# Token and channel mixer on one core: normalisation in the transposed layout, and a token product in 14 matmuls instead of 15

## Chip, cores and metric

The kernel runs on one core of one Trainium2 chip. The metric is device microseconds (us) of one execution, as the median of several runs; lower is better. The engines are named as the profile names them: PE (TensorE matmuls), PEld (TensorE weight loads), DVE (VectorE), ACT (ScalarE), POOL (GpSimd) and SP (SyncE, which here only issues DMAs).

## What is computed

Inputs are `q, k, v` of shape (8, 8, 576, 64): batch, heads, tokens, head size. The model width is 8 x 64 = 512.

```python
q_s = softmax over the head size of q;  k_s = softmax over the tokens of k
kv  = einsum('bhsd,bhse->bhde', k_s, v)
x   = einsum('bhsd,bhde->bhse', q_s, kv), heads side by side   # (8, 576, 512)
h   = max(x^T @ w_tok1, 0) @ w_tok2;   u = x + h^T              # over the tokens
y   = u + max(u @ w_ch1, 0) @ w_ch2                             # first channel layer, 512 -> 1536 -> 512
mu, var = mean and variance of y over the 512 channels
xn  = (y - mu) / sqrt(var + 1e-6) * g_ln
out = y + max(xn @ w2_ch1, 0) @ w2_ch2                          # second channel layer, 512 -> 2048 -> 512
```

The weight matrices come as 64-bit floats; the kernel turns them into 32-bit ones on the chip ("decode").

## The kernel before, in words

**Precision.** Every large product is made in three passes: an operand is split into a rounded part (hi) and the rest (lo), and hi·hi, hi·lo and lo·hi are summed (`PASSES`, L18). `split` (L136) makes the two parts: ACT copies to the rounded type, and DVE or POOL subtracts.

**Units.** A unit is one batch with two heads; there are 32. The 576 tokens of a unit lie as 4 chunks of 128 rows and a tail of 64 rows. `Unit.start` (L409) gives each step a tick. `q_split` (L507) makes hi and lo of the normalised q: one ACT copy and one POOL subtraction over 128 x 640. `tok1` (L533) is the token product of q with `w_tok1`: 3 passes x 5 chunks = 15 matmuls (L538), where the fifth chunk is the tail with 64 empty rows. `q_T` (L545) transposes q; for the 8 early units it transposes the hi and lo parts, and the tail takes two transposes (L570).

**Blocks.** The 4608 tokens are worked in 9 blocks of 512. Blocks 0 to 7 of the first channel layer (`Phase1`) are the first 512 tokens of a batch; block 8 is made of the eight 64-token tails. A block runs over 12 slices of the hidden width; each is 12 matmuls into a PSUM tile (`L1`, L684), a ReLU with split (ACT L141, DVE L142) and 12 matmuls into four accumulators (`L2`, L701), two slices later. The second channel layer (`Phase2`) does the same with 16 slices (L829 and L844). `finish` (L708) adds the residual into `yT`, which has channels on the partitions and tokens along the row: 4 DVE additions (L722), 4 POOL additions (L725). `y_store` (L628) turns `yT` chunk by chunk with 4 transposes on PE (L631), copies on ACT (L641), and writes to the DRAM tensor `y_dram`, which is in the order of the tokens.

**Norm.** For block j of the second layer `Norm` (L743) loads 512 consecutive tokens of `y_dram` with tokens on the partitions (L740), takes mean and variance with `bn_stats` and `bn_aggr` on DVE (L768, L770), the reciprocal root with a few small operations (L775 to L789), normalises on DVE (L793, four tensor_scalar), and then makes four turns: each turn is 4 transposes on PE (L804) into a PSUM tile, from which ACT (L809) writes the hi part and DVE (L810) the lo part, both scaled with g_ln. So there are 9 x 4 = 36 turns.

```python
later(at, self.load)
for i in range(CT // 2):
    later(at + 4 + i, call(self.stats, i))
    later(at + 9 + i, call(self.hat, i))
...
for kk in range(KD):
    later(at + turns + kk + kk // 2, call(self.turn, kk))
```

**Order of the work.** The order on each queue is written out by hand. `tick()` advances a counter, and `later(n, fn)` puts a step n ticks ahead. In the first layer a slice has four ticks, in the second two (after L1 and after L2), so a block of the second layer has about 32 ticks. The Norm of block 0 is started in the last block of the first layer, that of block j + 1 in block j. The weights of the second layer are decoded in 32 chunks (`Loads`, L259), 8 in the block before the last one of the first layer, the others up to the end of block 0 of the second layer: per chunk one SP load, four DVE operations (L100, L108, L115, L121), one on ACT (L129) and one on POOL (L130). The blocks of the second layer run 0 to 8. At their end `finish` (L851) adds the residual and POOL issues the output's DMA (SP for the last block).

Of the kernel before, what the change touches and what calls it, by code (L numbers as in the profile page):

```python
# [24 lines left out]
def kernel(  # L25
# [44 lines left out]
    CT = BLK // P  # L70
    LAG = 2
# [9 lines left out]
    y_dram = dram.tile([NT, DM], F32, name="y_dram")  # L81
# [54 lines left out]
    def split(x, hi, lo, engine):  # L136
        nc.scalar.activation(out=hi, in_=x, func=AF.Copy)  # L137
        engine.tensor_tensor(out=lo, in0=x, in1=hi.bitcast(F32), op=ALU.subtract)  # L138
# [71 lines left out]
    def tok1_chunk(c0, n, rows):  # L210
        def load():
            st = stage(n * T)[:rows]
            if c0 < NC:
                src = w_tok1[0:S0].rearrange("(p c) t -> p c t", c=NC)[:, c0:c0 + n]
            else:
                src = w_tok1[S0:S].rearrange("(p c) t -> p c t", c=1)
            nc.sync.dma_start(out=st.rearrange("p (c t) w -> p c (t w)", c=n), in_=src)
            return st

        def use(st):  # L220
            return decode(
                st, lambda x: x.rearrange("p (c t) -> p c t", c=n),
                w1[:rows, 0, c0:c0 + n], w1[:rows, 1, c0:c0 + n],
            )
# [176 lines left out]
    class Unit:  # L401
# [143 lines left out]
        def q_T(self, i):  # L545
# [18 lines left out]
            w = (c1 - c0) * P  # L564
            for xs in ((0, 1),) if 2 * w <= 512 else ((0,), (1,)):
                pq = psum("pq", True)
                for x in xs:
                    for c in range(c0, c1):
                        m = (x - xs[0]) * w + (c - c0) * P
                        nc.tensor.transpose(  # L570
                            out=pq[:, m:m + P].bitcast(F32R), in_=self.qn[:, x, c],
                            identity=spare[3][:, IDR:IDR + P],
                        )
                nc.scalar.activation(
                    out=self.qT[:, xs[0]:xs[-1] + 1, sl],
                    in_=pq[:, 0:len(xs) * w].rearrange("p (x s) -> p x s", x=len(xs))[:, :, 0:n],
                    func=AF.Copy,
                )
# [49 lines left out]
    def y_store(j, c):  # L628
# [13 lines left out]
        if j < B:  # L642
            dst = y_dram[j * S:j * S + S0, :].rearrange("(p c) d -> c p d", c=NC)[c]
            nc.scalar.dma_start(out=dst, in_=yn)
            return
        for i in range(P // R):
            b = c * (P // R) + i
            nc.scalar.dma_start(out=y_dram[b * S + S0:(b + 1) * S, :], in_=yn[i * R:(i + 1) * R])
# [7 lines left out]
    class Phase1:  # L656
# [51 lines left out]
        def finish(self):  # L708
# [19 lines left out]

            for c in range(CT):
# [7 lines left out]
    def load_y(j, pool):  # L737
        y = pool.tile([P, CT, DM], F32, tag="y", name="y")
        src = y_dram[j * BLK:(j + 1) * BLK, :]
        nc.sync.dma_start(out=y, in_=src.rearrange("(p c) d -> p c d", c=CT))  # L740
        return y

    class Norm:  # L743
        def __init__(self, j):
            self.j = j

        def start(self, at, turns=12):
# [4 lines left out]
            for i in range(CT // 2):  # L752
                later(at + 4 + i, call(self.stats, i))
                later(at + 9 + i, call(self.hat, i))
            later(at + 6, self.root)
            later(at + 8, self.rstd)
# [3 lines left out]
        def load(self):  # L760
            self.y = load_y(self.j, w2p[0])

        def stats(self, i):
            if i == 0:
                self.st = main.tile([P, CT, 6], F32, tag="st6", name="st6")
                self.mv = main.tile([P, CT, 2], F32, tag="mv", name="mv")
            for c in range(2 * i, 2 * i + 2):
                nc.vector.bn_stats(out=self.st[:, c], in_=self.y[:, c])  # L768
            for c in range(2 * i, 2 * i + 2):
                nc.vector.bn_aggr(out=self.mv[:, c], in_=self.st[:, c])  # L770

        def root(self):
            self.ve = main.tile([P, CT], F32, tag="ve", name="ve")
            self.r = main.tile([P, CT], F32, tag="r0", name="r0")
            nc.vector.tensor_scalar(  # L775
                out=self.ve, in0=self.mv[:, :, 1], scalar1=1e-6, scalar2=None, op0=ALU.add
            )
            later(1, lambda: nc.scalar.activation(out=self.r, in_=self.ve, func=AF.Sqrt))

        def rstd(self):  # L780
            ve, r0 = self.ve, self.r
            r1 = main.tile([P, CT], F32, tag="r1", name="r1")
            nc.vector.reciprocal(out=r0, in_=r0)
            nc.vector.tensor_tensor(out=r1, in0=r0, in1=r0, op=ALU.mult)
            nc.vector.tensor_tensor(out=r1, in0=r1, in1=ve, op=ALU.mult)
            nc.vector.tensor_scalar(
                out=r1, in0=r1, scalar1=-0.5, scalar2=1.5, op0=ALU.mult, op1=ALU.add
            )
            nc.vector.tensor_tensor(out=r0, in0=r0, in1=r1, op=ALU.mult)  # L789
# [243 lines left out]
```

## Time and profile before

| | us |
|---|---|
| median of 3 runs | 1674.12 (1673.66 to 1674.39) |
| the profiled execution | 1673.57 |
| span of its profile, first to last instruction | 1671.8 |
| PE busy in the span | 1642.0 (98%) |
| DVE, ACT, POOL busy | 644.3, 410.1, 318.5 |

The first 94 us are the early units; the first channel layer follows, with the other units between its matmuls, until about 855 us, and then the second layer. "Busy" counts the time in which an engine has at least one instruction at work. The chain of work that ended last is followed back from the last instruction of the kernel, at each step to what released it.

### The profile page before, as it was taken

The page shows a single profiled execution, that of the slowest core. Times are in us where ns is not written, and L with a number is a line of the kernel's source. Part 1 is how long each engine was busy: PE and PEld are TensorE (multiplying, and loading weights), DVE is VectorE, ACT ScalarE, POOL GpSimd, SP SyncE. Part 2 cuts the span into 40 slices and gives each one's busy share as a digit, 9 for nine tenths or more (in the row PEclk, how much of TensorE's full clock was granted, in tenths as well). Part 3 has the DMA queues.
Part 4 walks back from the last instruction along what each step waited for, and adds up shares of the span by engine and source line. Part 5 has one row for each costly group of instructions (what it writes and reads, how often), then busy time and mean ns, then how long its engine had stood idle before and what let it go on. Part 6 is the DMA issues. An engine that isn't in the chain of part 4 may idle for free.

```text
span 1671.8 us, 20195 instructions
## 1 busy us (share of the span) xinstructions
PE 1642.0 (98%) x8136; PEld 1380.9 (83%) x8136; DVE 644.3 (39%) x1290; ACT 410.1 (25%) x824; POOL 318.5 (19%) x244
## 2 busy tenths in 40 slices
PE   5999999999999999999999999999999999999998
PEld 4888888888888888888888888888888888888887
DVE  6875434344333434353557621222223131222211
ACT  4663333323232323321222211111111111111110
POOL 5743522232232313221223200000000000000000
PEclk9999999999999999999999999999999999999999
DMA  8552312121121212133225210101010101010010
GB/s 230 126 159 75 87 49 69 49 53 51 42 68 28 76 36 69 28 107 114 88 86 173 76 44 25 51 25 51 25 51 25 51 17 60 0 69 8 5 46 26
DMA packets 122062, 105.39 MB, mean 63 GB/s; under 512 B 92976, under 2 KB 101424, under 8 KB 118512
## 3 DMA queue, kind: packets, MB, share of 16 engines
q1 hardware_dynamic: 115568, 86.27, 17.9%
q10 hardware_dynamic: 5248, 9.44, 1.6%
q0 software_dynamic: 1152, 8.39, 1.2%
q8 instruction: 64, 1.05, 0.3%
q14 instruction: 30, 0.25, 0.0%
HBM read 82.05 MB, written 22.02 MB: 62 GB/s over the span
## 4 chain that ended last, share of the span: by engine, by line
PE 94%; DVE 2%; POOL 1%; issue 1%; ACT 1%; DMA 1%; SPq 0%; POOLq 0%; DVEq 0%; ACTq 0%
PE ph L829 24%; PE acc L844 24%; PE ph L684 17%; PE acc L701 17%; PE pu L601 4%; PE pg L538 3%; PE pk L514 2%; PE py L631 1%; PE px L804 1%; PE pq L559 1%; PE pq L586 1%; DMA rawq<-in_q 0%; DVE spare L138 0%; DVE dt L108 0%; POOL yT L725 0%
## 5 line engine op out<-in xcount | busy, mean ns | idle before, releaser
L142 DVE SCALAR_TENSOR_TENSOR h<-ph,h 128x512 fp32r<-128x512 f32 x252 | 174.0, 691 | 708.8 <-ACT h L141 708.7
L829 PE MATMUL ph<-xT,w 128*128 128x512 f32 x1728 | 420.2, 392 | 0.0
L844 PE MATMUL acc<-w,h 128*128 128x512 f32 x1728 | 420.0, 392 | 0.0
L829 PEld LDWEIGHTS ph<-xT,w 128*128 128x128 f32 x1728 | 323.0, 188 | 70.5 <-POOL w L130 0.2
L844 PEld LDWEIGHTS acc<-w,h 128*128 128x128 f32 x1728 | 322.9, 188 | 68.9
L141 ACT ACTIVATE h<-ph 128x512 fp32r<-128x512 f32 x252 | 150.5, 597 | 770.7 <-PE ph L829 587.0
L684 PE MATMUL ph<-u,w 128*128 128x512 f32 x1296 | 324.7, 395 | 0.0
L701 PE MATMUL acc<-h,w 128*128 128x512 f32 x1296 | 323.7, 394 | 0.0
L701 PEld LDWEIGHTS acc<-h,w 128*128 128x128 f32 x1296 | 237.1, 188 | 46.7
L684 PEld LDWEIGHTS ph<-u,w 128*128 128x128 f32 x1296 | 236.8, 188 | 46.7 <-DVE u L621 0.4
L859 POOL DMA_DIRECT2D out<-y x8 | 4.4, 556 | 635.8 <-DVE y L855 635.8
L467 POOL TENSOR_TENSOR qt<-rawq,qm 128x640 f32<-128x640 f32 x24 | 30.3, 1261 | 241.0 <-PE pt L461 95.5
L130 POOL TENSOR_TENSOR w<-t,w 128x512 fp32r<-128x512 f32 x32 | 41.9, 1310 | 152.8 <-ACT w L129 152.8
L538 PE MATMUL pg<-w,qn 128*128 128x256 f32 x480 | 63.8, 285 | 3.4 <-ACT w L137 3.4
L538 PEld LDWEIGHTS pg<-w,qn 128*128 128x128 f32 x480 | 62.0, 193 | 6.0 <-ACT w L137 3.7
L601 PE MATMUL pu<-w,hs 128*128 128x288 f32 x384 | 61.4, 295 | 0.0
L601 PEld LDWEIGHTS pu<-w,hs 128*128 128x128 f32 x384 | 54.4, 188 | 0.3 <-ACT hs L141 0.2
L138 DVE TENSOR_TENSOR qT<-pq,qT 128x512 fp32r<-128x512 f32 (+1 forms) x48 | 22.0, 458 | 76.1 <-ACT qT L137 76.1
L725 POOL TENSOR_TENSOR yT<-yT,u 128x512 f32<-128x512 f32 x32 | 43.0, 1359 | 37.9 <-DVE yT L722 37.9
L482 POOL TENSOR_TENSOR kt<-rawk,kb 128x640 f32<-128x640 f32 x24 | 38.1, 1587 | 40.8 <-ACT kb L478 40.8
L138 POOL TENSOR_TENSOR qn<-qt,qn 128x640 fp32r<-128x640 f32 x24 | 38.0, 1582 | 32.7 <-ACT qn L137 30.9
L129 ACT ACTIVATE w<-t 128x512 fp32r<-128x512 f32 x32 | 20.3, 633 | 97.0 <-DVE t L121 94.6
(140 smaller groups left out, 1243.3 us busy)
## 6 DMA issues: line engine op xcount, KB each, us to landing
y<-y_dram SPq DMA_DIRECT2D x18, 1024.0 KB, 4.8
st<-in_moe_w_ch SPq DMA_DIRECT2D x31, 512.0 KB, 3.8
vt<-in_v SPq DMA_DIRECT2D x64, 128.0 KB, 2.9
y_dram<-yn ACTq DMA_DIRECT2D x32, 256.0 KB, 2.4
out<-y POOLq DMA_DIRECT2D x8, 1024.0 KB, 4.1
rawk<-in_k SPq DMA_DIRECT2D x54, 128.0 KB, 2.8
rawq<-in_q SPq DMA_DIRECT2D x27, 256.0 KB, 3.1
stage<-in_moe_w_ch SPq DMA_DIRECT2D x10, 512.0 KB, 3.8
```

The source lines that it names most:

```text
L130: nc.gpsimd.tensor_tensor(out=lo, in0=x, in1=hi.bitcast(F32), op=ALU.subtract)
L138: engine.tensor_tensor(out=lo, in0=x, in1=hi.bitcast(F32), op=ALU.subtract)
L141: nc.scalar.activation(out=hi, in_=x, func=AF.Relu)
L142: nc.vector.scalar_tensor_tensor(out=lo, in0=x, scalar=0.0, in1=hi.bitcast(F32), op0=ALU.max, op1=ALU.subtract)
L482: nc.gpsimd.tensor_tensor(out=self.kt, in0=self.kr, in1=kb.to_broadcast([P, NC + 1, 2, D]), op=ALU.subtract,)
L538: nc.tensor.matmul(out=pg[:, 0:T], lhsT=self.qn[:, x, c], rhs=w1[:, y, c, :], start=(n == 0), stop=(n == len(terms) - 1),)
L601: nc.tensor.matmul(out=pu[:, 0:HN], lhsT=l, rhs=r, start=(n == 0), stop=(n == len(terms) - 1))
L684: nc.tensor.matmul(out=ps, lhsT=w[:, x, kk, fo:fo + P], rhs=u[:, y, kk], start=(n == 0), stop=(n == 3 * KD - 1),)
L701: nc.tensor.matmul(out=self.acc[dd], lhsT=w[:, x, f % 2, dd * P:(dd + 1) * P], rhs=h[:, y], start=(f == self.f0 and n == 0), stop=(f == se ...
L725: nc.gpsimd.tensor_tensor(out=yT[:, :, x], in0=yT[:, :, x], in1=u[:, 1, :, x].bitcast(F32), op=ALU.add)
L829: nc.tensor.matmul(out=ps, lhsT=w[:, x, kk, fo:fo + P], rhs=xT[:, y, kk], start=(n == 0), stop=(n == 3 * KD - 1),)
L844: nc.tensor.matmul(out=self.acc[c], lhsT=h[:, x, c * P:(c + 1) * P], rhs=w[:, y, f % 2], start=(f == 0 and n == 0), stop=(f == self.f1 - 1 ...
```

## The change

`tok1` and its tail. The 64 rows of the tail chunk that were empty now take the lo part of the tail: rows 0 to 63 hold hi, rows 64 to 127 hold lo, and the hi part of the tail of `w_tok1` is loaded a second time into rows 64 to 127. One matmul gives hi·hi + lo·hi of the tail, a second gives hi·lo, so a unit has 3 x 4 + 2 = 14. `q_split` is one ACT copy, a POOL subtraction over 128 x 512 and one over 64 x 128. An early `q_T` transposes the tail once.

Norm. `y_store` takes mean and variance from each stored chunk (`bn_stats`, `bn_aggr` on DVE, in the blocks of the first layer) into a tile `mr` that holds them for all 9 blocks. `yT` itself is stored to a DRAM tensor `yT_dram` (1 MB per block, an SP DMA 8 ticks after `finish`). A new class `Root` makes the reciprocal roots for several blocks at once (blocks 0 to 6 in block 7 of the first layer, blocks 7 and 8 in block 0 of the second), turns `mr` with one PE transpose, and stores it as rows to `mr_dram`. `Norm` loads `yT` and, in two halves of 256 tokens, mean and reciprocal root as rows sent to all 128 partitions; per half, DVE subtracts (128 x 1024) and POOL multiplies (128 x 1024). A turn is then only the ACT copy and the DVE operation, from SBUF. The second layer keeps the first layer's blocks, in the order 0 to 6, 8, 7; `y_dram` is laid out by block, and block 8 is written to the output by two DMAs of 64 partitions.

```diff
+    y_dram = dram.tile([NB, P, CT, DM], F32, name="y_dram")
+    yT_dram = dram.tile([NB, P, KD, BLK], F32, name="yT_dram")
+    mr_dram = dram.tile([NB, 2 * BLK], F32, name="mr_dram")
+    mr = main.tile([P, NB, 2, CT], F32, name="mr")
...
+            for r in (slice(0, R), slice(R, P)):
+                nc.sync.dma_start(
+                    out=st[r].rearrange("p t w -> p (t w)"), in_=w_tok1[S0:S]
+                )
...
-            split(self.qt, self.qn[:, 0], self.qn[:, 1], nc.gpsimd)
+            split(self.qt, self.qn[:, 0], self.qn[:, 1, 0:NC], nc.gpsimd)
+            nc.gpsimd.tensor_tensor(
+                out=self.qn[R:, 0, NC], in0=self.qt[:R, NC],
+                in1=self.qn[:R, 0, NC].bitcast(F32), op=ALU.subtract,
+            )
...
-            terms = [(x, y, c) for x, y in PASSES[0:2] for c in range(NC + 1)]
-            terms += [(1, 0, c) for c in range(NC + 1)]
+            terms = [(x, y, c) for x, y in PASSES for c in range(NC)] + [(0, 0, NC), (0, 1, NC)]
...
+        nc.scalar.dma_start(out=y_dram[j, :, c], in_=yn)
+        st = main.tile([P, 6], F32, tag="st6", bufs=2, name="st6")
+        nc.vector.bn_stats(out=st, in_=yn)
+        nc.vector.bn_aggr(out=mr[:, j, :, c], in_=st)
...
+            later(8, lambda: nc.sync.dma_start(out=yT_dram[self.j], in_=yT))
...
+    class Root:
+        def start(self, at):
+            for n, fn in zip((0, 1, 2, 3), (self.root, self.rstd, self.turn, self.store)):
+                later(at + 2 * n, fn)
...
+        def turn(self):
+            n = (self.j1 - self.j0) * 2 * CT
+            pm = psum("pm")
+            nc.tensor.transpose(
+                out=pm[:n, 0:P],
+                in_=mr[:, self.j0:self.j1].rearrange("p j x c -> p (j x c)"), identity=ident,
+            )
+            self.rows = main.tile([P, P], F32, tag="mrr", name="mrr")[:n]
+            nc.scalar.activation(out=self.rows, in_=pm[:n, 0:P], func=AF.Copy)
...
     class Norm:
...
             later(at, self.load)
+            for i in range(2):
+                later(at + 4 * i, call(self.load_b, i))
+                later(at + 4 * i + 4, call(self.hat, i))
             for kk in range(KD):
                 later(at + turns + kk + kk // 2, call(self.turn, kk))
...
+        def load_b(self, i):
+            self.b = w2p[0].tile([P, 2, HB], F32, tag="mrb", name="mrb")
+            src = mr_dram[self.j].rearrange("(x n) -> x n", x=2)[:, i * HB:(i + 1) * HB]
+            nc.sync.dma_start(out=self.b, in_=src.partition_broadcast(P))
+
         def hat(self, i):
-            for c in range(2 * i, 2 * i + 2):
-                nc.vector.tensor_scalar(
-                    out=self.y[:, c], in0=self.y[:, c], scalar1=self.mv[:, c, 0:1],
-                    scalar2=self.r[:, c:c + 1], op0=ALU.subtract, op1=ALU.mult,
-                )
+            y = self.y[:, :, i * HB:(i + 1) * HB]
+            mu, r = (self.b[:, x:x + 1].to_broadcast([P, KD, HB]) for x in range(2))
+            nc.vector.tensor_tensor(out=y, in0=y, in1=mu, op=ALU.subtract)
+            nc.gpsimd.tensor_tensor(out=y, in0=y, in1=r, op=ALU.mult)
...
         def turn(self, kk):
...
-            pt = psum("px")
-            for c in range(CT):
-                nc.tensor.transpose(
-                    out=pt[:, c * P:(c + 1) * P],
-                    in_=self.y[:, c, kk * P:(kk + 1) * P], identity=ident,
-                )
-            g = gT[:, kk:kk + 1]
-            nc.scalar.activation(out=self.xT[:, 0, kk], in_=pt, func=AF.Copy, scale=g)
+            g, y = gT[:, kk:kk + 1], self.y[:, kk]
+            nc.scalar.activation(out=self.xT[:, 0, kk], in_=y, func=AF.Copy, scale=g)
             nc.vector.scalar_tensor_tensor(
-                out=self.xT[:, 1, kk], in0=pt, scalar=g, in1=self.xT[:, 0, kk].bitcast(F32),
+                out=self.xT[:, 1, kk], in0=y, scalar=g, in1=self.xT[:, 0, kk].bitcast(F32),
                 op0=ALU.mult, op1=ALU.subtract,
             )
...
-        for j in range(NB):
+        ORDER = [*range(B - 1), B, B - 1]
+        for j in ORDER:
...
+                        Root(0, B - 1).start(30)
...
-                    later(16, o.load)
-                    if o.j + 1 < NB:
-                        Norm(o.j + 1).start(14 if o.j == 0 else 8)
+                    later(18, o.load)
+                    if o.j == 0:
+                        Root(B - 1, NB).start(26)
+                    if o.j != ORDER[-1]:
+                        Norm(ORDER[ORDER.index(o.j) + 1]).start(15 if o.j == 0 else 8)
```

## Rows read from the trace of the kernel before

**Rows 1.** The page: busy time of each engine, and the granted TensorE clock in 40 slices.

```profile
PE 1642.0 (98%) x8136; PEld 1380.9 (83%) x8136; DVE 644.3 (39%) x1290; ACT 410.1 (25%) x824; POOL 318.5 (19%) x244
...
PEclk9999999999999999999999999999999999999999
```

**Rows 2.** The page: the chain that ended last, its shares by line.

```profile
PE ph L829 24%; PE acc L844 24%; PE ph L684 17%; PE acc L701 17%; PE pu L601 4%; PE pg L538 3%; PE pk L514 2%; PE py L631 1%; PE px L804 1%; PE pq L559 1%; PE pq L586 1%; DMA rawq<-in_q 0%; DVE spare L138 0%; DVE dt L108 0%; POOL yT L725 0%
```

**Rows 3.** Busy time by stretch: us, then PE, PEld, DVE, ACT, POOL (instructions), clock, DMA share, GB/s.

```profile
20.00:40.00 20.00, 14.71 (x88) 13.54 (x88) 15.67 (x38) 12.42 (x29) 16.52 (x14) 1.00 0.91 264
60.00:80.00 20.00, 17.56 (x150) 17.07 (x149) 17.12 (x42) 13.19 (x34) 14.96 (x11) 1.00 0.57 147
438.00:532.00 94.00, 94.00 (x521) 81.06 (x520) 37.48 (x85) 28.77 (x64) 27.82 (x20) 1.00 0.21 53
853.00:943.00 90.00, 90.00 (x411) 73.88 (x410) 67.14 (x110) 23.48 (x42) 28.09 (x21) 1.00 0.43 135
1391.00:1481.00 90.00, 90.00 (x404) 73.93 (x403) 21.81 (x42) 12.32 (x21) 0.53 (x1) 1.00 0.10 36
```

**Rows 4.** The chain in a late block: start, us, what; first and last of the turns.

```profile
1539.83 2.72 PE ph L829 x12
1542.55 0.44 PE px L804 x4
...
1558.02 2.04 PE ph L829 x9
```

**Rows 5.** Groups of instructions on PE: busy us, mean ns, idle before.

```profile
L538 PE MATMUL pg<-w,qn 128*128 128x256 f32 x480 | 63.8, 285 | 3.4 <-ACT w L137 3.4
...
L804 PE MATMUL px<-ident,y 128*128 128x128 f32 x144 | 21.6, 272 | 0.0
```

**Rows 6.** The chain in the first layer: a unit's token product, and one single transpose.

```profile
194.89 1.77 PE pg L538 x15
...
200.85 0.11 PE pt L461
```

**Rows 7.** The chain at the early units' end: token product, tail transposes, first layer.

```profile
87.47 1.73 PE pg L538 x15
...
91.54 0.12 PE pq L570 x2
...
94.32 0.69 PE ph L684 x3
```

**Rows 8.** Groups on POOL: busy us, mean ns, idle before and its releaser.

```profile
L130 POOL TENSOR_TENSOR w<-t,w 128x512 fp32r<-128x512 f32 x32 | 41.9, 1310 | 152.8 <-ACT w L129 152.8
...
L138 POOL TENSOR_TENSOR qn<-qt,qn 128x640 fp32r<-128x640 f32 x24 | 38.0, 1582 | 32.7 <-ACT qn L137 30.9 <-DMA rawq<-in_q 1.8
...
L138 POOL TENSOR_TENSOR w<-more,w 128x128 fp32r<-128x128 f32 x1 | 0.5, 467 | 0.0
```

**Rows 9.** Groups on DVE: Norm's statistics and its normalisation.

```profile
L768 DVE BATCH_NORM_STATS2 st<-y 128x6 f32<-128x512 f32 x36 | 22.8, 676 | 4.9 <-DMA y<-y_dram 4.9
...
L793 DVE TENSOR_SCALAR y<-y,mv,r 128x512 f32<-128x512 f32 x36 | 19.9, 596 | 0.3
```

**Rows 10.** DVE in order of time, block 0 of the second layer.

```profile
908.85 1.29 DVE L768 BATCH_NORM_STATS2 st<-y 128x6 f32<-128x512 f32 x2 [3.33 <-DMA y<-y_dram]
...
925.88 0.68 DVE L115 SCALAR_TENSOR_TENSOR t<-st,t 128x512 uint32<-128x512 uint32 x1
...
928.20 1.68 DVE L115 SCALAR_TENSOR_TENSOR t<-st,t 128x512 uint32<-128x512 uint32 x1
```

**Rows 11.** POOL in order of time, the same stretch.

```profile
928.04 1.29 POOL L130 TENSOR_TENSOR w<-t,w 128x512 fp32r<-128x512 f32 x1 [4.32 <-ACT w L129]
```

**Rows 12.** Weight loads of PE in order of time, the same stretch.

```profile
937.13 0.76 PEld L829 LDWEIGHTS ph<-xT,w 128*128 128x128 f32 x4 [0.24 <-POOL w L130]
```

**Rows 13.** DMA issues: queue, count, KB each, median us from issue to landing.

```profile
y<-y_dram SPq DMA_DIRECT2D x18, 1024.0 KB, 4.8
...
u<-u_dram SPq DMA_DIRECT2D x1, 2048.0 KB, 9.6
```

More of the change, by code (lines that the diff above doesn't have):

```diff
@@ L70 @@
     CT = BLK // P
+    HB = BLK // 2
     LAG = 2
@@ L735, with __init__, root, rstd @@
     ln_t = {}
[L737 to L741, printed above, removed]
+    class Root:
+        def __init__(self, j0, j1):
+            self.j0, self.j1 = j0, j1
+        def start(self, at):
+            for n, fn in zip((0, 1, 2, 3), (self.root, self.rstd, self.turn, self.store)):
+                later(at + 2 * n, fn)
+        def root(self):
+            n = self.j1 - self.j0
+            self.ve = main.tile([P, NB, CT], F32, tag="ve", name="ve")[:, 0:n]
+            self.r = mr[:, self.j0:self.j1, 1]
+            nc.vector.tensor_scalar(
+                out=self.ve, in0=self.r, scalar1=1e-6, scalar2=None, op0=ALU.add
+            )
+            nc.scalar.activation(out=self.r, in_=self.ve, func=AF.Sqrt)
+        def rstd(self):
+            ve, r0 = self.ve, self.r
+            r1 = main.tile([P, NB, CT], F32, tag="r1", name="r1")[:, 0:self.j1 - self.j0]
+            nc.vector.reciprocal(out=r0, in_=r0)
+            nc.vector.tensor_tensor(out=r1, in0=r0, in1=r0, op=ALU.mult)
+            nc.vector.tensor_tensor(out=r1, in0=r1, in1=ve, op=ALU.mult)
+            nc.vector.tensor_scalar(
+                out=r1, in0=r1, scalar1=-0.5, scalar2=1.5, op0=ALU.mult, op1=ALU.add
+            )
+            nc.vector.tensor_tensor(out=r0, in0=r0, in1=r1, op=ALU.mult)
+        def turn(self):
+            n = (self.j1 - self.j0) * 2 * CT
+            pm = psum("pm")
+            nc.tensor.transpose(
+                out=pm[:n, 0:P],
+                in_=mr[:, self.j0:self.j1].rearrange("p j x c -> p (j x c)"), identity=ident,
+            )
+            self.rows = main.tile([P, P], F32, tag="mrr", name="mrr")[:n]
+            nc.scalar.activation(out=self.rows, in_=pm[:n, 0:P], func=AF.Copy)
+        def store(self):
+            dst = mr_dram[self.j0:self.j1].rearrange("j (x p) -> (j x) p", p=P)
+            nc.sync.dma_start(out=dst, in_=self.rows)
     class Norm:
@@ L819, in load @@
         def load(self):
-            self.y = load_y(self.j, main)
+            self.y = main.tile([P, CT, DM], F32, tag="y", name="y")
+            nc.sync.dma_start(out=self.y, in_=y_dram[self.j])
         def L1(self, f, mid):
@@ L851, in finish @@
         def finish(self):
-            y = self.y
-            dst = out[self.j * BLK:(self.j + 1) * BLK, :].rearrange("(p c) d -> p c d", c=CT)
+            y, last = self.y, self.j == ORDER[-1]
+            if self.j < B:
+                dst = out[self.j * S:self.j * S + S0, :].rearrange("(p c) d -> p c d", c=CT)
+                dst = [(slice(0, P), dst)]
+            else:
+                dst = out.rearrange("(b s) d -> s b d", s=S)[S0:S]
+                n = P // R
+                dst = [
+                    (slice(i * R, (i + 1) * R), dst.rearrange("s (c i) d -> i s c d", i=n)[i])
+                    for i in range(n)
+                ]
             for c in range(CT):
                 nc.vector.tensor_tensor(out=y[:, c], in0=self.acc[c], in1=y[:, c], op=ALU.add)
-                if self.j == NB - 1:
-                    nc.sync.dma_start(out=dst[:, c], in_=y[:, c])
-            if self.j < NB - 1:
-                nc.gpsimd.dma_start(out=dst, in_=y)
+                if last:
+                    for p, x in dst:
+                        nc.sync.dma_start(out=x[:, c], in_=y[p, c])
+            if not last:
+                for p, x in dst:
+                    nc.gpsimd.dma_start(out=x, in_=y[p])
     with tc.manual_schedule():
```

81 lines of the change are left out of this document (21 added, 60 removed).

## Prediction

> **What bounds it.** I read the page's busy line first: PE is at work for 1642.0 of 1671.8 us, at the full granted clock in every slice [rows 1]. A busy PE proves little by itself, so the chain that ended last came next: its shares are nearly all PE lines, and both kinds of instruction that the change takes out stand among them, the transposes of Norm (px L804) and the token product (pg L538) [rows 2]. The table by stretch says where this holds [rows 3]. From 438 to 532 us and from 1391 to 1481 us PE has no idle time at all, while DVE is busy for 37.5 of 94 and 21.8 of 90 us and POOL for 27.8 and 0.5: there a microsecond less on PE is a microsecond less of time, and work on DVE and POOL is hidden. Two stretches differ. In the early units (20 to 40 us) PE is busy for 14.7 of 20 us only, POOL for 16.5, and the DMA engines for 0.91 of the time. In block 0 of the second layer (853 to 943 us) PE is full, but DVE has 67 of 90 us, and near its end PE waits 0.24 us for a decoded weight [rows 12]: the decode arrives just in time there, with no slack.
>
> **Norm's transposes.** Their mean of 272 ns [rows 5] is a latency, since matmuls overlap; what they cost is read from the chain. From the first turn at 1542.55 to the piece at 1558.02 lie 15.47 us, with four turns and five groups of 12 matmuls [rows 4]. An undisturbed group takes 2.72 us, five take 13.60, so four turns cost 1.87, or 0.467 us each (the 0.44 of the row and a slightly later restart behind it). There are 144 transposes, 36 turns: **-16.8 us**. Root brings two transposes in their place, at 0.11 each [rows 6]: **+0.2**.
>
> What the turns are replaced by lies beside PE. Per block: a 1 MB load of yT instead of one of y, 4.8 us [rows 13]; two loads of rows to all partitions, 256 KB each; two subtractions and two multiplications over 128 x 1024. Neither size is in the trace. A POOL operation of 512 elements takes 1.31 and one of 640 takes 1.58 us [rows 8], which extrapolates to 2.4 and doubles to 2.6; I take 2.6. The subtraction is twice the 0.68 of a DVE operation with two SBUF inputs [rows 10], 1.3. For the load I take 3 us, between 2.4 (half of 4.8 for a quarter of the bytes) and the slowest row at hand, 9.6 [rows 13]. Load, two halves (the second load waits for the first multiplication, as they share a buffer) and four turns of about 0.7 us make 4.8 + 2 x 3.9 + 3 + 2.8, some 18 us, within the 24 ticks (24 x 2.72 = 65 us) that remain of a block: hidden, except in block 0. The SP queue waits behind that second load, but in blocks 1 and later only loads with ticks to spare stand behind it. The statistics move to the first layer, where the same 36 `bn_stats` at 0.68 us [rows 9] find a DVE busy for 40%; they wait for the ACT copy that follows the same tick's transposes, and the ReLU behind them has two slices in hand. The 1 MB store of yT makes SP wait for POOL's additions, before loads that have 10 ticks of lead; DMA is at 0.21 there. The two output DMAs of block 8 are not in the last block. All of this is costed at nothing; were the cover gone, the price would be that of the rivals below.
>
> **Token product.** 15 matmuls take 1.77 us [rows 6], one 0.118. For the 24 units that run between full-PE matmuls: **-2.8 us**. In the 8 early units PE would save 8 x 0.115, and 8 x 0.06 for a tail transpose [rows 7], 1.4 us, but PE is not the bound there. Against it: the tail is loaded twice, 128 KB more in a stretch that moves 264 GB/s [rows 3], 0.5 us; and POOL gets a second, small subtraction. That is bounded by nothing and by the 0.47 us of a 128 x 128 one, less the 0.27 that 512 instead of 640 elements save [rows 8]: at most +0.2 per unit, 1.6 in all. Ends -1.4 and +2.1; as chain and engines alternate there, I take a value a little on the PE side: **-0.4**.
>
> **Block 0 of the second layer.** Decode and Norm(1) share DVE and POOL. A DVE operation with two SBUF inputs that takes 0.68 us alone took 1.68 when it began while POOL's subtraction (928.04 to 929.33) ran [rows 10, 11]: it stood until POOL had finished. Two multiplications of 2.6 can thus hold the decode on DVE for 5.2 us. Three removed turns ahead of the waiting weight load bring PE's need forward by 1.4. In return DVE loses 4 x 0.68 of statistics and 4 x 0.60 of normalisation and gets 2 x 1.3, 2.5 us less [rows 9]. If POOL always blocks: 5.2 + 1.4 - 2.5 = 4.1 us of stall; if never, none. DVE also idles here, 3.33 us for the load of y alone [rows 10], and part of POOL's time falls into such gaps and on ReLUs that read PSUM. I take a third: **+1.2**. Ends: -0.2 (today's wait goes) and +6.6 (no relief).
>
> The Trainium skill, "SBUF — State Buffer", section "Who interferes with whom", has the rule: a DVE instruction with two SBUF inputs and a GpSimd instruction that reads SBUF exclude each other for their whole length. The trace agrees (1.68 against 0.68 us). By durations alone block 0 would cost nothing and the sum below would give 1654.3; by the rule in full it gives 1658.4.
>
> **Sum.** -16.8 + 0.2 - 2.8 - 0.4 + 1.2 = -18.6, on the profiled execution's 1673.57: 1655.0. That execution lies 0.55 below the median of the runs, 1674.12, so the median should come to **1655.5 us**.
>
> **Rivals.** (a) Decode-bound block 0: POOL's multiplications and the earlier need meet in full, 4.1 to 6.6 instead of 1.2. For it: DVE 67 of 90 and no slack [rows 3, 12]. Against: less DVE work, and DVE's order is fixed by the same ticks. Time 1658.4 to 1660.9. The rule of the page above would make this one.
> (b) The early units lose: second tail load and second POOL subtraction lie on the chain, +2.1 instead of -0.4: 1658.0. For it: DMA 0.91 and POOL 16.5 of 20 us. Against: the tail's terms are now the last two of 14, so the first unit's product waits later for them than the 3.4 us that it waits now [rows 5].
> (c) Slower than before: the rows sent to all partitions arrive late in every block. Two loads of L us and 11 us of work must fit in 65, so nothing happens below L = 27; from there each further us costs two per block, 16 over eight blocks; at L = 29 the kernel is at 1655.5 + 32 = 1687.5. Against: 2 MB take 9.6 us [rows 13].
> (d) The change takes the transposes away and PE's time comes back as idle, as xT is ready no sooner: about 1674. Against: 21.8 and 0.5 us of DVE and POOL in 90 [rows 3].
>
> **Numbers.** Forecast 0.68, (a) 0.14, (b) 0.12, (c) 0.02, (d) 0.04. About 0.2% (3.3 us) is what a measurement of this kernel can tell from no change; the forecast, (a) and (b) are faster by more: 0.94, same 0.04, slower 0.02. The range starts at all gains at their ends, -16.8 + 0.2 - 2.8 - 1.4 - 0.2 = -21.0, 1652.6 on the profiled execution, taken as 1652.5, and reaches 1660.0, which takes in (b) and most of (a).
>
> **What would show it.** No px line; pg x448; PE busy down by about 20 us with an idle time of about 30 us as before. A late block's period shorter by 1.87 us. POOL with two operations of about 2.6 us per block of the second layer. In block 0, a wait of PE's weight loads for POOL's or ACT's w of 1 to 2 us: 4 or more means (a). The first matmul of L684, at 94.3 us on the chain now [rows 7], half a microsecond sooner: a later one means (b). A wait of L829 for xT at the start of blocks means (c) or (d), and that the forecast is wrong.

## The result, and the profile after

The changed kernel takes **1656.73 us** (median of 4 runs, 1655.01 to 1657.32) beside 1674.24 (4 runs, 1673.66 to 1674.39) for the kernel before on the same chip: a ratio of 0.9895, 95% interval 0.9881 to 0.9908. The forecast of 1655.5 us is 1.2 too low, and its range holds the result. The profiled execution took 1655.01 us, the lowest of the four; with a span of 1653.2 it is 18.6 us shorter than the profiled one before. That this is the forecast sum to the tenth is luck, as the stretches below show.

The page's busy line and clock answer to [rows 1]:

```profile
PE 1621.5 (98%) x7954; PEld 1361.1 (82%) x7954; DVE 647.0 (39%) x1230; ACT 407.9 (25%) x819; POOL 370.2 (22%) x295
...
PEclk9999999999999999999999999999999999999999
```

PE is at work for 20.5 us less, and its idle time is 31.7 us, against 29.8 before. The work taken out of PE has therefore left the time. In the groups on PE the row of px is gone and pg has 448 matmuls, 32 fewer, as 32 units with 14 give; Root brings the two pm. Answering to [rows 5]:

```profile
L553 PE MATMUL pg<-w,qn 128*128 128x256 f32 x448 | 59.5, 284 | 2.9 <-ACT w L142 1.5 <-POOL w L144 1.0 <-POOL qn L144 0.5
...
L781 PE MATMUL pm<-ident,mr 128*16 128x128 f32 x1 | 0.3, 273 | 0.0
L781 PE MATMUL pm<-ident,mr 128*56 128x128 f32 x1 | 0.3, 270 | 0.4 <-DVE mr L776 0.4
```

The chain in a late block, where [rows 4] had four turns between the groups, is now one group of 12 behind another, with nothing between them:

```profile
1528.47 2.72 PE ph L850 x12
1531.19 2.72 PE acc L865 x12
1533.91 2.72 PE ph L850 x12
```

To see where the gain comes from I cut each profiled execution at three landmarks on PE: the first matmul of the first channel layer (where the early units end), the last matmul `pu` of the units, and the first matmul of the second layer. Each is the start of a first or last instruction in the trace.

| stretch, us | before | after | forecast | found |
|---|---|---|---|---|
| early units | 94.16 | 92.71 | -0.4 | -1.45 |
| the other 24 units | 624.5 | 622.0 | -2.8 | -2.5 |
| from there to the second layer | 136.6 | 136.7 | -1.76 | +0.1 |
| second layer | 816.5 | 801.8 | -13.65 | -14.7 |

The forecast column splits the sum by place: -1.87 for one turn group and 0.11 for one transpose of Root stand in the third row, eight of the former, one of the latter and block 0's +1.2 in the last. So one stretch gained nothing where 1.8 was due, and two gained more. The waits of PE tell of the first. The kernel before has no such wait for h, and no pm:

```profile
PE ph L694 <- DVE h L150: 0.9, 1, 0.9
...
PE pm L781 <- DVE mr L776: 0.4, 1, 0.4
```

Both lie in that stretch, and each has its reason in the trace. **The first** is in the last block of the first layer, while the Norm of block 0 runs. In order of time:

```profile
828.36 1.23 DVE L821 TENSOR_TENSOR yT<-yT,mrb 128x1024 f32<-128x1024 f32 x1 [2.46 <-DMA mrb<-mr_dram]
829.51 0.69 DVE L120 SCALAR_TENSOR_TENSOR t<-st,t 128x512 uint32<-128x512 uint32 x1
829.67 2.78 POOL L822 TENSOR_TENSOR yT<-yT,mrb 128x1024 f32<-128x1024 f32 x1 [4.04 <-DVE yT L821]
830.23 2.77 DVE L126 SCALAR_TENSOR_TENSOR t<-st,t 128x512 uint32<-128x512 uint32 x1
...
833.03 0.63 ACT L134 ACTIVATE w<-t 128x512 fp32r<-128x512 f32 x1 [9.96 <-DVE t L126]
833.57 1.07 ACT L149 ACTIVATE h<-ph 128x512 fp32r<-128x512 f32 x2
...
834.18 0.69 DVE L150 SCALAR_TENSOR_TENSOR h<-ph,h 128x512 fp32r<-128x512 f32 x1 [1.18 <-ACT h L149]
...
834.92 3.06 PE L694 MATMUL ph<-u,w 128*128 128x512 f32 x12 [0.92 <-DVE h L150]
```

The decode's L126 starts 0.56 us after POOL's multiplication and ends half a microsecond behind it, 2.77 us instead of 0.69: it was held until POOL had ended. ACT's queue has the decode's copy (L134) ahead of the ReLU (L149): the copy waits for L126, the ReLU waits behind the copy, DVE's half of the ReLU waits for that, and PE waits 0.92 us for it. DVE was late already, since it had stood 2.46 us for the rows from `mr_dram`. POOL has a part in that too: the second load of rows shares its buffer with the first, and SP issues it just as POOL's first multiplication ends:

```profile
821.40 2.79 POOL L822 TENSOR_TENSOR yT<-yT,mrb 128x1024 f32<-128x1024 f32 x1 [7.39 <-DVE yT L821]
...
824.22 0.37 SPq L816 DMA_DIRECT2D mrb<-mr_dram  x1
```

**The second** is Root's chain, one block earlier:

```profile
762.23 1.28 ACT L765 ACT_TABLE_LOAD   x1
...
762.86 0.17 DVE L762 TENSOR_SCALAR ve<-mr 128x28 f32<-128x28 f32 x1
...
763.53 0.23 ACT L765 ACTIVATE mr<-ve 128x28 f32<-128x28 f32 x1
...
763.79 0.33 DVE L770 RECIPROCAL mr<-mr 128x28 f32<-128x28 f32 x1 [0.76 <-ACT mr L765]
...
764.81 0.19 DVE L776 TENSOR_TENSOR mr<-mr,r 128x28 f32<-128x28 f32 x1
...
765.14 0.27 PE L781 MATMUL pm<-ident,mr 128*56 128x128 f32 x1 [0.38 <-DVE mr L776]
```

ACT loads a table for the square root (1.28 us), five small DVE operations follow, and the transpose stands in PE's queue 4 ticks after the first step; a tick there is about half a group of 2.72 us, so it comes before its input. The four ticks make 5.4 us back from 764.76, where the transpose is due, to 759.3 (an estimate); yet Root's first operation starts at 762.86 only, as decode and ReLU operations stand ahead of it on DVE.

### The profile page after: what moved, and what is told of

The parts are those of the page before. It is cut to its first block, busy times and chain, and to the rows that moved or that the text cites. A ratio compares the mean times of both kernels' runs of the same rounds, so it can differ in the third digit from the quotient of the medians.

```text
span 1653.2 us, 19900 instructions
## 1 busy us (share of the span) xinstructions
PE 1621.5 (98%) x7954; PEld 1361.1 (82%) x7954; DVE 647.0 (39%) x1230; ACT 407.9 (25%) x819; POOL 370.2 (22%) x295
## 4 chain that ended last, share of the span: by engine, by line
PE 90%; DVE 3%; DMA 2%; POOL 2%; ACT 1%; issue 1%; SPq 1%; POOLq 0%; DVEq 0%; ACTq 0%
PE ph L850 24%; PE acc L865 24%; PE ph L694 16%; PE acc L711 16%; PE pu L614 4%; PE pg L553 3%; PE pk L530 2%; PE py L644 1%; PE pq L574 1%; PE pq L599 1%; DVE t L120 1%; DMA mrb<-mr_dram 1%; DVE t L126 1%; DMA rawq<-in_q 0%; DMA more<-in_moe_w_ch 0%
## 5 line engine op out<-in xcount | busy, mean ns | idle before, releaser
L149 ACT ACTIVATE h<-ph 128x512 fp32r<-128x512 f32 x252 | 150.3, 597 | 786.0 <-PE ph L850 614.6
L822 POOL TENSOR_TENSOR yT<-yT,mrb 128x1024 f32<-128x1024 f32 x18 | 43.9, 2437 | 252.5 <-issue 180.3
L553 PE MATMUL pg<-w,qn 128*128 128x256 f32 x448 | 59.5, 284 | 2.9 <-ACT w L142 1.5
L553 PEld LDWEIGHTS pg<-w,qn 128*128 128x128 f32 x448 | 57.6, 191 | 5.4 <-issue 1.7
L134 ACT ACTIVATE w<-t 128x512 fp32r<-128x512 f32 x32 | 20.3, 633 | 108.6 <-DVE t L126 108.2
```

The source lines that it names most:

```text
L149: nc.scalar.activation(out=hi, in_=x, func=AF.Relu)
L553: nc.tensor.matmul(out=pg[:, 0:T], lhsT=self.qn[:, x, c], rhs=w1[:, y, c, :], start=(n == 0), stop=(n == len(terms) - 1),)
L822: nc.gpsimd.tensor_tensor(out=y, in0=y, in1=r, op=ALU.mult)
```

## Experiments

Each ratio is to runs of the kernel before on the same chip: for e1 to e4 1674.35 (11 runs), for e5 to e8 1673.72 (7 runs), for e9 to e11 1674.89 (7 runs), on three different chips.

| | median us (lowest to highest, runs) | ratio, 95% interval |
|---|---|---|
| e1 token product only | 1669.64 (1668.71 to 1670.86, 7) | 0.9972, 0.9961 to 0.9983 |
| e2 Norm only | 1659.44 (1658.88 to 1659.84, 4) | 0.9911, 0.9896 to 0.9926 |
| e3 changed kernel again | 1655.95 (1654.76 to 1656.48, 4) | 0.9888, 0.9875 to 0.9902 |
| e4 multiply on DVE | 1655.19 (1654.66 to 1655.67, 4) | 0.9885, 0.9871 to 0.9898 |
| e5 first unit filled | 1655.50 (1654.27 to 1656.35, 4) | 0.9890, 0.9875 to 0.9905 |
| e6 Root spaced | 1654.88 (1654.15 to 1655.63, 4) | 0.9886, 0.9869 to 0.9902 |
| e7 Norm later | 1655.82 (1653.32 to 1658.84, 4) | 0.9893, 0.9878 to 0.9908 |
| e8 e4 and e6 | 1653.85 (1651.85 to 1655.08, 4) | 0.9879, 0.9865 to 0.9894 |
| e9 e4, e5 and e6 | 1654.26 (1653.69 to 1655.22, 4) | 0.9880, 0.9863 to 0.9896 |
| e10 changed kernel again | 1655.65 (1655.24 to 1656.00, 4) | 0.9886, 0.9871 to 0.9901 |
| e11 tail loaded once | 1656.22 (1655.81 to 1656.84, 4) | 0.9890, 0.9875 to 0.9905 |

The medians of two programs that differ by less than a microsecond can't be told apart by these. The stretches of the profiled executions can:

| stretch, us | before | after | e1 | e2 | e3 | e4 | e5 | e6 | e7 | e8 | e9 | e10 | e11 |
|---|---|---|---|---|---|---|---|---|---|---|---|---|---|
| early units | 94.2 | 92.7 | 93.7 | 94.8 | 92.7 | 94.2 | 92.4 | 94.1 | 91.5 | 94.9 | 93.5 | 93.9 | 94.6 |
| other units | 624.5 | 622.0 | 621.5 | 624.0 | 622.0 | 621.9 | 621.9 | 621.9 | 621.9 | 621.9 | 621.9 | 621.9 | 621.9 |
| to the second layer | 136.6 | 136.7 | 136.6 | 136.6 | 136.5 | 135.5 | 136.6 | 135.9 | 136.5 | 134.8 | 134.9 | 136.6 | 136.7 |
| second layer | 816.5 | 801.8 | 816.4 | 801.7 | 801.8 | 801.6 | 801.6 | 801.6 | 801.7 | 801.6 | 801.6 | 801.8 | 801.9 |

The same program repeats its last three stretches within 0.2 us (after, e3, e10), while its early units end between 92.7 and 93.9. A difference in the last three rows is the edit's; one in the first need not be.

**The two halves alone: e1 and e2.** e1 is the kernel before with the token part of the diff; e2 is the changed kernel with that part undone. The core of e1's edit, which e2 makes the other way round:

```diff
-            terms = [(x, y, c) for x, y in PASSES[0:2] for c in range(NC + 1)]
-            terms += [(1, 0, c) for c in range(NC + 1)]
+            terms = [(x, y, c) for x, y in PASSES for c in range(NC)] + [(0, 0, NC), (0, 1, NC)]
...
```

> The kernel before with the token part of the change alone (14 matmuls, second load of the tail, second POOL subtraction, one tail transpose in the early units); Norm as before. Theory A, PE counts in the early units too: 32 x 0.115 to 0.118 + 8 x 0.06 = 4.2 us less, so 1670.0 us against 1674.2. Theory B, the prediction's step, PE is not the bound in the early units: 2.8 + 0.4 = 3.2 less, 1671.0. Theory C, the second tail load and the second POOL subtraction lie on the chain: 0.7 less, 1673.5. The first matmul of L684's counterpart tells A from B and C by itself: 1.4 us sooner, 0.4 sooner, or later.

> The changed kernel with its token part undone. Theory A: the Norm part gives 36 x 0.467 - 0.2 = 16.6 us on PE, less the new waits of PE that the changed kernel's trace shows in the last two blocks of the first layer (0.9 for a late DVE part of a ReLU, 0.4 to 0.8 for Root's transpose), so 1674.2 - 15.2 = 1659 in a run like the profiled one, 1660.5 in the middle of the others. Theory B, that token part and Norm part share what they free (as by a common wait): 1657 or less, the token part then adding nothing on top.

e1 lies 4.7 us below before in the median, e2 14.9 (1674.35 less each); together 19.6, against 18.4 for both in e3, so the halves add within the spread. By stretches e1 has 0.5 less in the early units, 3.0 less in the 24 units and nothing behind them, which is theory B, although its median lies lower than even theory A's 1670.0. e2 has 14.8 less in the second layer and nothing in the stretch ahead of it, theory A. It also has 0.5 less in the 24 units, for which no run gives a reason. PE's two new waits stand in e2 as well (0.8 for h, 0.4 for mr): they belong to Norm and Root, not to the token product.

**The changed kernel again: e3 and e10.** No edit.

> The changed kernel once more, for its spread: its four runs lie between 1655.0 and 1657.3, those of the kernel before between 1673.7 and 1674.4. Theory A, the spread is made by the loads that Norm of block 0 now waits for in the last block of the first layer: the wait of PE for the ReLU's DVE part there is longer than 0.9 us in a slower run, by as much as the run is longer, and the early units end at 92.9 us as before. Theory B, it is made in the early units, whose loads are the densest: the first matmul of the first layer moves by 1 to 2 us, the wait stays 0.9.

> The changed kernel, to compare with the two others on the same chip: 1655.0 to 1657.3, the first layer's begin anywhere from 92 to 95 us, the stretch between the last unit and the second layer at 136.6 us and the second layer at 801.8 us, as in its two traces.

1655.95 and 1655.65, both lower than the 1656.73 of the first four runs. The median of all 12 runs of this program is 1655.8. The traces speak for theory B: the wait for h is 0.8 us in both, and it is the early units that differ.

**The multiplication on DVE: e4.** If POOL's multiplication holds DVE, DVE does better to do it itself.

```diff
-            nc.gpsimd.tensor_tensor(out=y, in0=y, in1=r, op=ALU.mult)
+            nc.vector.tensor_tensor(out=y, in0=y, in1=r, op=ALU.mult)
```

> The changed kernel with the multiplication of the normalisation on DVE instead of POOL, all else alike. Theory A, POOL's multiplication holds off the decode operation on DVE (2.77 us for one of 0.69), ACT waits for that operation and the ReLU stands behind it on ACT: without POOL the 0.9 us wait of PE goes, DVE's 0.69 is back, 0.5 to 1.0 us less than the changed kernel. Theory B, DVE is late there because of its own work and the row loads that it waits for: two more operations of 1.2 us on DVE make PE's wait longer, about 2 us, and the time 1 us more.

The stretch becomes 1.2 us shorter (135.5; against e3 and e10 it is 1.0 and 1.1), and PE waits for no h there. The same moments of e4, in order of time:

```profile
823.94 0.37 SPq L816 DMA_DIRECT2D mrb<-mr_dram  x1
...
827.98 1.23 DVE L821 TENSOR_TENSOR yT<-yT,mrb 128x1024 f32<-128x1024 f32 x1 [0.62 <-DMA mrb<-mr_dram]
829.24 1.23 DVE L822 TENSOR_TENSOR yT<-yT,mrb 128x1024 f32<-128x1024 f32 x1
...
831.10 0.69 DVE L126 SCALAR_TENSOR_TENSOR t<-st,t 128x512 uint32<-128x512 uint32 x1
```

The units of e4 end 1.4 us later than those of after (716.1 and 714.7), so, counted from the end of the units, L126 is done 2.6 us sooner (at 831.79, against 833.00 plus 1.4). Two things make up the 2.6. Multiplying costs DVE 1.23 us where being held beside POOL cost it 2.08 (2.77 less 0.69): 0.8. And the second subtraction begins 1.8 us sooner, since the first multiplication frees the buffer sooner and DVE waits 0.62 us instead of 2.46 for the rows. So e4 shows what the multiplication on POOL cost here, but not how much of it by the hold and how much by the late load; a kernel with a second buffer for the rows would tell, and was not run. In the second layer it changes 0.2 us at most: there the work is hidden on either engine.

**More time for Root: e6, and both edits: e8.**

```diff
-            for n, fn in zip((0, 1, 2, 3), (self.root, self.rstd, self.turn, self.store)):
+            for n, fn in zip((0, 2, 4, 5), (self.root, self.rstd, self.turn, self.store)):
```

> The changed kernel with Root's four steps at 0, 4, 8 and 10 ticks instead of 0, 2, 4 and 6. Theory A, PE waits in block 7 of the first layer since the chain root, table load, square root, four DVE operations has two ticks too few: the wait of 0.4 us on PE before the transpose (0.8 in the weight loads) goes, and the time after the early units is shorter by 0.5 to 0.8 us. Theory B, the wait follows DVE's backlog of decode operations and moves along: no difference.

> Both of the earlier edits: the multiplication on DVE and Root's steps spaced. Theory A, their waits are apart from each other, so the gains add: 1.3 us for the one (measured after the early units) and 0.5 to 0.8 for the other, 1654.0 to 1654.5 in the median, or 1655.0 when the early units are at their slower level. Theory B, what one wait frees the other takes: no better than the multiplication on DVE alone, 1655.2.

e6 shortens the stretch by 0.7, and the wait of pm is gone. e8 shortens it by 1.9 in all, to 134.8: this is the -1.8 that the forecast had there. In e8's chain no wait stands where the 0.92 us were:

```profile
832.75 2.72 PE acc L711 x12
835.47 2.72 PE ph L694 x12
```

With 1653.85 e8 is the fastest version by its median. The chips differ by 1.2 us in the kernel before, so each version is set against its own: 19.9 us less for e8, 19.2 for e10 and 18.4 for e3. By medians the two edits are thus worth 0.6 to 1.5, which fits the 1.9 of the stretch only loosely. The early units of e8's profiled run were the longest of all (94.9), so that execution's own time, 1655.08, doesn't show the gain.

**Norm five ticks later: e7.** This asks how much slack the second layer has.

```diff
-                        Norm(ORDER[ORDER.index(o.j) + 1]).start(15 if o.j == 0 else 8)
+                        Norm(ORDER[ORDER.index(o.j) + 1]).start(15 if o.j == 0 else 13)
```

> The changed kernel with Norm started 5 ticks (about 13.6 us) later in the blocks of the second layer from block 1 on. Theory A, the prediction's: load, row loads, subtractions, multiplications and turns take some 18 us of the 65 that remain, so a block's period stays the same and the time too (within 0.3 us in the trace from the first layer's begin on). Theory B, the chain was near the end of the block: each of 7 blocks pays, 7 us and more in all.

The second layer takes 801.7, the same. Loads, subtraction, multiplication and turns have at least 5 ticks, 13.6 us, to spare. The low execution (1653.32) is one with early units of 91.5, the high one (1658.84) has no trace.

**The early units: e5, e9 and e11.** In the first profile the granted clock fell at 28 us, where PE now waits three times for its first token product, and I took this for the cause of the spread. e5 keeps PE at work there with 20 matmuls whose weights are zero, and e9 does so on top of e8. e11 takes the tail of `w_tok1` from DRAM once and copies the hi part to rows 64 to 127 on ACT. The edit of e5, and then that of e11:

```diff
             for n, (x, y, c) in enumerate(terms):
+                for _ in range({12: 12, 13: 8}.get(n, 0) if self.n == 0 else 0):
+                    nc.tensor.matmul(out=pg[:, 0:T], lhsT=spare[3][:, 12 * P:13 * P], rhs=w1[:, 0, 0, :], start=False, stop=False)
...
+        nc.scalar.activation(out=spare[3][:, 12 * P:13 * P], in_=ident, func=AF.Copy, scale=0.0)
```

```diff
-            for r in (slice(0, R), slice(R, P)):
-                nc.sync.dma_start(
-                    out=st[r].rearrange("p t w -> p (t w)"), in_=w_tok1[S0:S]
-                )
+            else:
+                src = w_tok1[S0:S].rearrange("(p c) t -> p c t", c=1)
+            nc.sync.dma_start(out=st.rearrange("p (c t) w -> p c (t w)", c=n), in_=src)
...
+                    nc.scalar.activation(
+                        out=w1[R:, 0, NC], in_=w1[:R, 0, NC].bitcast(F32), func=AF.Copy
+                    )
```

> The changed kernel with 20 more matmuls of a zero weight tile in the token product of the first unit, 12 in front of the thirteenth and 8 in front of the last, where PE stood still for 1.5 and 1.0 us; they add nothing to the sums. In all traces of kernels with the 14 matmuls the granted clock is at 0.50 of full from about 28 us, for 7 us in some runs and for 10 us with a second fall at 44 to 48 us in others; with the 15 matmuls it falls only at 42 to 47 us. Theory A, the standing still in the first unit brings the fall at 28 us, and the falls make the spread: with PE at work there the fall at 28 us is gone, the first layer begins at 92.7 us or sooner in every run, and the median comes down from 1656.0 to 1654.8 or less. Theory B, the fall comes from something else: the clock falls at about 28 us as before, the 20 matmuls cost nothing or up to 2 us, and the median is 1656 to 1658.

> Multiplication on DVE, Root's steps spaced, and the zero matmuls in the first unit together. Theory A, the clock's falls make a part of the early units' spread: early units as in the run with the zero matmuls (92.4 us), the rest as in the run with the two other edits (716.8 to 851.6 us between the last unit and the second layer, 134.8), so 1652.5 in the profile's run, and a median of 1653.0 or less against 1653.9 for the two edits alone. Theory B, the spread is in the loads and not in the clock: the median is 1653.9 as for the two edits, with as wide a spread.

> The changed kernel with the tail of the token weight loaded once and its hi part copied on ACT to rows 64 to 127 (one more operation of about 0.4 us there). Theory A, the second load of 128 KB lies on the chain of the early units, whose first 40 us move 190 to 290 GB/s: the first layer begins 0.5 us sooner than in the changed kernel's runs beside it, the median is 0.5 lower. Theory B, the early units are held by the chain through ACT, DVE and POOL, and the load is hidden: no difference, or 0.4 us later by the copy.

e5 has no fall of the clock in its trace (rows in the last section), and its early units take 92.4, the 92.7 of after less 0.3; that is well inside the 1.2 by which the early units of one program differ. Its four runs still spread over 2.1 us, but only the traced one is known to be without a fall: its mean granted clock is 1.000, that of the others 0.998 and 0.999. And e9, with the same 20 matmuls, has a fall at 42 to 46 us. So in both traces the 20 matmuls take away the fall at 28 us; what that fall costs, and whether the falls make the spread, these runs don't show. By its median e9 can't be told from e8: 20.6 us less than its kernel before, against 19.9. e11 gains nothing either: 1656.22 beside the 1655.65 of e10, with early units of 94.6. Nothing here speaks for the second load of the tail as what holds them. These three are misses; what makes the early units of one program end up to a few microseconds apart stays open.

## Why the prediction was right, and where its steps were off

**Norm's transposes, -16.8: right.** Eight of the nine groups of turns lie in the second layer, 8 x -1.87 = -14.96. With Root's second transpose, +0.11, that is -14.85, and -14.6 to -14.9 was found in every kernel that has the change (after, e2 to e11). The ninth group lies in the stretch ahead of it; e8 shows its gain.

**What replaces them, costed at nothing: right in the second layer, wrong ahead of it.** The sizes, first the groups after:

```profile
L822 POOL TENSOR_TENSOR yT<-yT,mrb 128x1024 f32<-128x1024 f32 x18 | 43.9, 2437 | 252.5 <-issue 180.3 <-DVE yT L821 72.2
L821 DVE TENSOR_TENSOR yT<-yT,mrb 128x1024 f32<-128x1024 f32 x18 | 24.2, 1342 | 5.9 <-DMA mrb<-mr_dram 5.9
```

then the DMA issues:

```profile
yT<-yT_dram SPq DMA_DIRECT2D x9, 1024.0 KB, 4.8
...
mrb<-mr_dram SPq DMA_DIRECT2D x18, 256.0 KB, 5.1
```

The multiplication took 2.44 where 2.6 was taken, the subtraction 1.34 against 1.3. The rows sent to all partitions took 5.1 us where 3 was taken, inside the bounds of 2.4 and 9.6: a quarter of the bytes of the load of yT, but no less time. That is 4.2 us more per block in a slack of which e7 used 13.6, so it cost nothing where the cover was there. Rival (c), which needed 27 us a load, is ruled out by this row.

**Where it failed: "All of this is costed at nothing", said also of the first layer's last two blocks.** The prediction looked for the clash of POOL's multiplication with the decode in block 0 of the second layer alone. The Norm of block 0 runs a block earlier, and the decode is at work there too. What POOL's multiplication did to DVE there, by the hold and by the late second load of rows, cost 1.0 to 1.2 us (e4). The step on Root counted its two transposes and none of what feeds them: table load, root and the DVE operations around it in 4 ticks, behind a busy DVE, 0.7 us (e6). Together 1.9 (e8; 1.7 and 1.8 against e3 and e10).

**Block 0, +1.2: wrong, about 0.1.** DVE is held, as expected. DVE, then POOL, then PE's weight loads, each in order of time:

```profile
904.93 2.34 DVE L821 TENSOR_TENSOR yT<-yT,mrb 128x1024 f32<-128x1024 f32 x1 [0.77 <-DMA mrb<-mr_dram]
...
907.80 2.29 DVE L105 TENSOR_SCALAR st<-st 128x512 f32<-128x512 f32 x1
...
916.64 2.33 DVE L821 TENSOR_TENSOR yT<-yT,mrb 128x1024 f32<-128x1024 f32 x1
...
919.50 2.49 DVE L120 SCALAR_TENSOR_TENSOR t<-st,t 128x512 uint32<-128x512 uint32 x1
```

```profile
904.90 1.29 POOL L135 TENSOR_TENSOR w<-t,w 128x512 fp32r<-128x512 f32 x1 [3.02 <-DMA mrb<-mr_dram]
907.41 2.40 POOL L822 TENSOR_TENSOR yT<-yT,mrb 128x1024 f32<-128x1024 f32 x1 [1.21 <-DVE yT L821]
...
919.05 2.39 POOL L822 TENSOR_TENSOR yT<-yT,mrb 128x1024 f32<-128x1024 f32 x1 [1.16 <-DVE yT L821]
...
930.63 1.30 POOL L135 TENSOR_TENSOR w<-t,w 128x512 fp32r<-128x512 f32 x1 [2.02 <-ACT w L134]
```

```profile
931.98 0.77 PEld L850 LDWEIGHTS ph<-xT,w 128*128 128x128 f32 x4 [0.31 <-POOL w L135]
```

Beside POOL's two multiplications, two decode operations took 1.9 us (2.29 for the usual 0.42) and 1.8 us (2.49 for 0.69) longer: 3.7, where the prediction allowed up to 5.2. Both subtractions took 1.1 longer as well (2.34 and 2.33 for 1.23), each beside a decode subtraction on POOL (at 904.90 and 916.59). The relief on DVE was smaller than counted, as the statistics of the first layer's last block still run in block 0: DVE is busy for 70.8 of its first 88.6 us, holds included, against 66.1 before. Yet the weight loads wait 0.31 us where they waited 0.24 [rows 12], and PE has no idle time.

What covers this is a lead that the decode gains earlier in the block. Two of POOL's decode subtractions before, the 25th of the 32 chunks and the 30th, for which the weight loads wait:

```profile
913.39 1.28 POOL L130 TENSOR_TENSOR w<-t,w 128x512 fp32r<-128x512 f32 x1 [8.10 <-ACT w L129]
...
935.79 1.29 POOL L130 TENSOR_TENSOR w<-t,w 128x512 fp32r<-128x512 f32 x1 [2.02 <-ACT w L129]
```

Counted from the first matmul of the second layer (at 855.3 before and 851.4 after), the 25th starts at 58.1 us before and at 53.5 after (904.90 above), 4.6 sooner. Before, the 3.33 us that DVE stood for the load of y and the first 1.29 us of statistics [rows 10] came ahead of this chunk on DVE; after, neither does. The 30th starts at 80.5 before and at 79.2 after (930.63): the holds and DVE's added work have used up 3.3 of the 4.6, and the 1.3 that are left are as much as PE's need came forward (81.8 to 80.6). So the prediction was right that the decode arrives just in time, but the idle 3.33 us, which it named without a number, paid for the holds. This is read from one execution of each kernel, and no run tests it; the wait is 0.31 and 0.30 in e3 and e10.

In the first layer's last block the held operation, late already, was the last one before the ReLU's turn on ACT, and no such lead was left. So the Trainium skill, "SBUF — State Buffer", section "Who interferes with whom", has the lock right in both places (2.77 for 0.69, 2.49 for 0.69). The time that the prediction worked out from its full price, rival (a), did not come: here a lock cost time only where what it held up had no slack.

**Token product, -2.8: right.** Over the 24 units the kernels with both parts show -2.5 or -2.6, the token part alone -3.0 (e1), and from e2 to after it is -2.0; the -2.8 lies among them. The chain shows one, against 1.77 for 15 in [rows 6]:

```profile
193.37 1.65 PE pg L553 x14
```

POOL's second subtraction took 0.474 us, the upper bound named. It lies on POOL and cost PE nothing in these units.

**Early units, -0.4: neither shown nor refuted.** Eight profiled executions have the changed early units (after, e1, e3, e4, e6, e7, e8, e10). They end between 91.5 and 94.9, with a median of 93.8; two have those of before, with 94.2 and 94.8 (e2). A difference of 0.4 can't be read from that. Rival (b), +2.1, would have put most of them above 96, and none is. Rival (d) is ruled out by PE's 20.5 us less work at 1.9 us more idle time.

**The step to the median.** Taking 0.55 us between profiled execution and median from the kernel before did not carry over: the first four runs of the changed kernel spread over 2.3 us, with the profiled one lowest, and put it at 1.7. Over its 12 runs (median 1655.8) the forecast is off by 0.3.

So the sum came out right because errors nearly cancel: 1.9 lost ahead of the second layer, where nothing was priced, and 0.3 less in the 24 units, against 1.1 that block 0 did not cost and 1.0 more from the early units of that one execution.

## What to carry to other kernels

Where PE is full, a transpose taken off it is worth its pitch in the chain (here 0.117 us each), not its mean duration. When work moves from PE to DVE or POOL, look for the clash at every place where the moved step runs, the first instance in an earlier stage too, and follow the held instruction through the in-order queue of each engine behind it up to PE. A POOL operation over two large SBUF operands beside a busy DVE may be dearer than the same work on DVE itself (1.23 us against 2.08 of being held).

## What was unexpected

**The clock in the early units.** The 40 slices of the page hide that the granted clock falls there to half, the lower of its two levels (1.2 instead of 2.4 GHz). Busy time by stretch of 2 us, columns as in [rows 3]; the last three columns are the granted clock, the DMA share and GB/s. Before, and then after:

```profile
28.00:30.00 2.00, 2.00 (x12) 2.00 (x13) 1.92 (x4) 0.62 (x3) 2.00 (x2) 1.00 1.11 330
...
44.00:46.00 2.00, 2.00 (x12) 2.00 (x11) 0.68 (x4) 0.68 (x2) 2.00 (x2) 0.50 0.62 140
```

```profile
26.00:28.00 2.00, 0.36 (x1) 0.19 (x1) 1.44 (x4) 2.00 (x4) 1.78 (x2) 0.92 1.02 347
28.00:30.00 2.00, 1.48 (x10) 1.48 (x10) 1.06 (x4) 1.75 (x5) 2.00 (x3) 0.50 0.97 338
...
44.00:46.00 2.00, 2.00 (x20) 2.00 (x19) 1.89 (x7) 1.70 (x4) 1.67 (x2) 1.00 0.71 190
```

Then e5, and last e10, the same program as after:

```profile
26.00:28.00 2.00, 1.93 (x17) 1.76 (x16) 1.41 (x4) 2.00 (x4) 1.71 (x2) 1.00 1.02 356
28.00:30.00 2.00, 1.94 (x18) 1.73 (x16) 1.32 (x4) 1.93 (x6) 2.00 (x2) 1.00 0.94 324
...
44.00:46.00 2.00, 2.00 (x19) 2.00 (x19) 1.88 (x7) 1.60 (x4) 1.67 (x2) 1.00 0.75 200
```

```profile
28.00:30.00 2.00, 1.84 (x11) 1.65 (x12) 0.96 (x3) 1.73 (x5) 2.00 (x2) 0.52 1.03 362
...
44.00:46.00 2.00, 2.00 (x11) 2.00 (x10) 1.32 (x3) 2.00 (x5) 1.48 (x2) 0.50 0.75 210
```

Before falls once, at 42 to 46 us; after once, at 28 to 34, following 2 us in which PE was busy for 0.36; e10 at both places; e5, whose PE has work from 26 to 30, nowhere. Over all traces with the token part, the early units end at 92.4 with no fall (e5), at 91.5 to 93.5 with one (after, e3, e7, e9) and at 93.7 to 94.9 with two (the others). The later fall divides them best: with it, at 42 to 48 us, the early units end at 93.5 or later in all nine traces that have it (before and e2 too), without it at 92.7 or sooner in the other four (after, e3, e5, e7). So the 1.45 us that after gained here came with the absence of that fall, and not clearly with the change. What is cause and what effect is open: a longer wait of PE could bring the fall as well as follow from one. And the mean granted clock of an execution does not order the times: runs of the changed kernel took 1656.48 at 0.999 and 1655.58 at 0.996.

**One-input operations are held too.** L105, a tensor_scalar with one SBUF input, took 2.29 instead of 0.42 us when it began 0.39 us into POOL's multiplication (907.80 and 907.41 above). The prediction counted operations with two inputs alone. The section of the Trainium skill named above has this as well: it lists tensor_scalar among the operations that can take the shared ports in a two-port mode. In which mode L105 ran, no trace here shows.

**A load of rows to all partitions** took as long here as a plain load of four times its bytes (medians of 5.1 and 4.8 us above).
